# Agent attention and a rational feed-forward block: batch 0's products with v in two halves of TensorE's columns, w_out's second quarter decoded later, and the last decoding step of w_out on GpSimd

## The chip, the cores and the metric

The kernel runs on one core of a Trainium2 chip. The metric is the device time of one execution in microseconds; lower is better. The engines are named as the profile names them: PE (matrix products; PEld its weight loads), DVE (VectorE), ACT (ScalarE), POOL (GpSimd) and SP (it only issues DMAs here). PSUM is the memory that PE writes its products to.

## The reference

```python
def _attn_ref(q, k, v, agents):              # B=2, N=12480, C=128, 49 agents
    def sm(a, b):
        s = scale * (a @ b.transpose(0, 2, 1))
        e = np.exp(s - s.max(-1, keepdims=True))
        return e / (e.sum(-1, keepdims=True) + 1e-09)
    agent_v = sm(agents, k) @ v              # 49 x 128 for each batch
    return sm(q, agents) @ agent_v

def _moe_ref(x, w_in, w_out, a, b):          # x: 24960 x 128, d_ff = 2048
    h = x @ w_in
    P = a[0] + a[1]*h + a[2]*h**2 + a[3]*h**3
    Q = 1.0 + abs(b[0])*abs(h) + abs(b[1])*h**2
    return (P / (Q + 1e-6)) @ w_out
```

q, k, v and agents are float32; w_in and w_out are float64, and the kernel turns them into float32 on the chip.

## The kernel before

**Two parts.** A first part (0 to about 57 us of the profiled execution) finds agent_v of batch 0 and decodes three quarters of the weights. Then every engine reads `flag` and branches into `main`, which runs all tokens of both batches through attention and the feed-forward block (to 1235 us), and does batch 1's agent_v beside it.

**agent_v of batch 0.** The 12480 keys are 98 chunks of 128, in groups g of 10 (the last has 8). PE makes the scores, DVE the maxima, ACT the exponentials S. `pv_pe` multiplies a group's chunks with v (49 x 129, the last column a sum) and adds them up in PSUM: groups 0 to 4 into `bank[4]` (HG = 5), 5 to 9 into `bank[5]`, which have different maxima; L863 scales the first by `fac`, L866 adds the second. `av_norm` (L289 to L291) divides, PE transposes (L294), ACT and DVE copy the result into `avt` (L297, L298). Each float32 product is two PE instructions in the profile.

**Decoding the weights.** A quarter is 512 columns, ("i", 0..3) of w_in, ("o", 0..3) of w_out. `decode` gives four steps: two ACT instructions (L177, L178), three of DVE (L181 to L183: t, t, s), two of POOL (L186: r = r * s; L187: r = r + t), and a last one of DVE (L190: dst = (z >= TINY2) * r). `ORDER` lists the loads on SP's queue among those of v and q, `DECS` the group after which a quarter is decoded; `dec` issues the last step of a quarter only after the first steps of the next one (`pend`). Quarters ("o", 0) and ("o", 1) fall in the stretch of agent_v; ("o", 2) and ("o", 3) are decoded in `main` by `w_stream`. In the branch taken here (`fast`), POOL also multiplies each quarter of w_out by a coefficient Kg (`w_scale`, L680).

**The attention of the first 1024 tokens** stands in the same stretch: scores after g = 2, exponentials, sums, `q_split` on POOL (L441 to L443), and the transposes `q_tr` on PE (L448) after g = 7.

**main.** x is never formed: m = agent_v * w_in (L301) is rounded to a high part by ACT (L304) and a rest by DVE (L309), and h is made from the attention weights and the two parts of m (L495, L496 on PE) in units of 3 x (128 of d_ff x 512 tokens). A unit then takes ACT (L560 and, for two units together, a logarithm and an exponential L574, L576), DVE (L589, L581), POOL (L601, a DMA that adds a constant from `omd` to u; L643, a product) and PE (L503, product with w_out) seven units later. `omd` is filled once at main's start: POOL writes a tile (L610), SP sends it (L611). The attention of later tokens, the decoding of ("o", 2) and ("o", 3) and batch 1 are cut into pieces that `attend` puts between the units. Up to unit 7 PE runs dummy products (L657).

**What sets the order.** The order on each engine is that in which the code issues; waits are by semaphores. A core's engines each work strictly through their own list.

## Time and profile before

| | us |
|---|---|
| three executions | 1233.75, 1234.26, 1234.34 (median 1234.26) |
| the profiled execution | 1236.99, of which its span 1235.2 |
| PE busy | 1203.0 (97%) |
| DVE, ACT, POOL busy | 1109.9 (90%), 1139.0 (92%), 1092.1 (88%) |

The span runs from the first to the last instruction of the profiled execution. PEclk, where it stands, is the granted clock of TensorE as a share of full speed: 1.00 is 2.4 GHz, 0.50 is 1.2 GHz.

### The profile page before, as it was taken

How to read it: one execution, taken by the hardware profiler on the slowest of the kernel's cores; microseconds unless marked ns; L12 is line 12 of the kernel's file. 1: busy time of each engine (PE TensorE's matmuls, PEld its weight loads, DVE VectorE, ACT ScalarE, POOL GpSimd, SP SyncE). 2: the span in 40 equal slices, each digit the busy share in tenths (PEclk: the TensorE clock that was granted, in tenths of full speed). 3: DMA queues.
4: the chain of work that ended last, by engine and by line, in shares of the span. 5: the costliest groups of instructions: out<-in, count | busy, mean ns of one | idle time of the engine just before them, and what ended most of it. 6: DMA issues, size and time to landing. Idle time of an engine off the chain costs nothing.

```text
span 1235.2 us, 14434 instructions
## 1 busy us (share of the span) xinstructions
PE 1203.0 (97%) x5396; PEld 706.7 (57%) x5396; DVE 1109.9 (90%) x876; ACT 1139.0 (92%) x717; POOL 1092.1 (88%) x544
## 2 busy tenths in 40 slices
PE   7979999999999999999999999999999999999998
PEld 7845555555555555555556555555555555555554
DVE  6898898988988888888989999999999998999996
ACT  3489999999999999999999999999999999999994
POOL 4549979798999989989798999999899998999993
PEclk8989999999999999999999999999999999999999
DMA  9569999898999989999899989999999989999991
GB/s 357 225 150 203 200 226 224 191 230 182 210 204 215 230 192 213 207 212 199 169 188 187 207 178 203 191 204 200 190 197 192 218 164 194 196 211 176 202 198 36
DMA packets 55312, 246.17 MB, mean 199 GB/s; under 512 B 4800, under 2 KB 5312, under 8 KB 55232
## 3 DMA queue, kind: packets, MB, share of 16 engines
q0 software_dynamic: 32768, 188.75, 79.5%
q1 hardware_dynamic: 22464, 56.39, 12.8%
q8 instruction: 45, 0.74, 0.2%
q14 instruction: 35, 0.29, 0.1%
HBM read 231.56 MB, written 13.57 MB: 198 GB/s over the span
## 4 chain that ended last, share of the span: by engine, by line
PE 63%; DVE 17%; DMA 6%; POOL 5%; issue 4%; ACT 4%; SPq 0%; DVEq 0%; ACTq 0%; POOLq 0%
PE outb L503 36%; PE slot L495 11%; PE slot L496 10%; DVE w L589 7%; DVE u L581 6%; POOL u L643 4%; DMA u<-omd 4%; ACT u L560 3%; PE outb L214 2%; DMA k<-kT 2%; PE outb L448 1%; PE outb L272 1%; ACT w L576 1%; POOL u L601 1%; DMA v<-vP 1%
## 5 line engine op out<-in xcount | busy, mean ns | idle before, releaser
L643 POOL TENSOR_TENSOR u<-u,w 128x1536 f32<-128x1536 f32 x240 | 906.4, 3985 | 14.5 <-DMA u<-omd 13.8
L503 PE MATMUL outb<-u,wo 128*128 128x512 f32 (+1 forms) x1568 | 712.9, 590 | 2.8 <-DVE av_two L278 1.3
L589 DVE SCALAR_TENSOR_TENSOR w<-slot,cf,u 128x1536 f32<-128x1536 f32 (+1 forms) x262 | 472.1, 1802 | 86.4 <-ACT u L560 66.6
L581 DVE SCALAR_TENSOR_TENSOR u<-u,cf,slot 128x1536 f32<-128x1536 f32 (+1 forms) x262 | 472.2, 1802 | 9.3
L503 PEld LDWEIGHTS outb<-u,wo 128*128 128x128 f32 x1568 | 295.3, 189 | 278.1 <-issue 242.4
L560 ACT ACTIVATE u<-slot 128x1536 f32<-128x1536 f32 (+1 forms) x262 | 380.0, 1451 | 44.1 <-PE slot L496 18.0
L495 PE MATMUL slot<-pT,m_hi 113*128 113x512 f32 (+3 forms) x800 | 370.5, 464 | 11.5 <-DVE u L581 10.5
L574 ACT ACTIVATE w<-w,cf 128x3072 f32<-128x3072 f32 (+1 forms) x134 | 374.3, 2795 | 0.5 <-DVE w L589 0.5
L576 ACT ACTIVATE w<-w 128x3072 f32<-128x3072 f32 (+1 forms) x134 | 361.9, 2703 | 0.0
L496 PE MATMUL slot<-pT,m_lo 113*128 113x512 f32 (+3 forms) x800 | 312.6, 392 | 0.0
L495 PEld LDWEIGHTS slot<-pT,m_hi 113*128 113x128 f32 x800 | 151.0, 189 | 88.2 <-DVE u L581 38.5
L601 POOL DMA_DIRECT2D u<-omd x112 | 158.5, 1415 | 31.0 <-DVE u L581 15.2
L496 PEld LDWEIGHTS slot<-pT,m_lo 113*128 113x128 f32 x800 | 151.8, 190 | 49.4 <-issue 25.3
L448 PEld LDWEIGHTS outb<-ident,p 128*113 128x113 f32 x187 | 26.2, 177 | 27.8 <-issue 14.7
L646 POOL COPY turn<-u 1x1 f32<-1x1 f32 x17 | 4.1, 241 | 41.4 <-DVE u L594 41.4
L594 DVE SCALAR_TENSOR_TENSOR u<-u,cf,w 128x1536 f32<-128x1536 f32 (+2 forms) x22 | 38.2, 1758 | 0.0
L214 PEld LDWEIGHTS outb<-ag,q 128*64 128x64 f32 x748 | 24.3, 140 | 18.1 <-issue 13.5
L448 PE MATMUL outb<-ident,p 128*113 128x128 f32 x187 | 28.7, 276 | 2.8 <-POOL p L443 2.3
L441 POOL TENSOR_TENSOR e<-e,qs 128x392 f32<-128x392 f32 (+1 forms) x25 | 29.6, 1183 | 0.1
L442 POOL TENSOR_SCALAR p<-e 128x392 fp32r<-128x392 f32 (+1 forms) x25 | 29.5, 1180 | 0.1
L214 PE MATMUL outb<-ag,q 128*64 128x49 f32 x748 | 27.3, 227 | 0.0
L186 POOL TENSOR_TENSOR r<-r,s 128x512 f32<-128x512 f32 x6 | 9.3, 1556 | 19.6 <-DVE s L183 19.6
(137 smaller groups left out, 520.1 us busy)
## 6 DMA issues: line engine op xcount, KB each, us to landing
u<-omd POOLq DMA_DIRECT2D x112, 1536.0 KB, 12.3
q<-qT SPq DMA_DIRECT2D x24, 512.0 KB, 8.6
outT<-o SPq DMA_DIRECT2D x48, 256.0 KB, 5.9
u<-omd POOLq DMA_DIRECT2D x16, 768.0 KB, 8.3
v<-vP SPq DMA_DIRECT2D x24, 258.0 KB, 8.3
k<-kT SPq DMA_DIRECT2D x24, 256.0 KB, 7.6
v<-vP SPq DMA_DIRECT2D x9, 645.0 KB, 11.4
k<-kT SPq DMA_DIRECT2D x8, 640.0 KB, 9.5
```

Of the source, the lines that this page charges most:

```text
L214: PE.matmul(bank[lo:hi, o:o + A], lhsT=toks[:, lo:hi], rhs=ag[:, b * A:(b + 1) * A], start=True, stop=True)
L448: PE.transpose(bank[:KR, c * CH:(c + 1) * CH], t[:, h * 4 + c, :].bitcast(F32), ident[:CH, :CH])
L495: PE.matmul(s[:, j, lo:hi], lhsT=m_hi[b][:KR, f], rhs=rhs, start=True, stop=False)
L496: PE.matmul(s[:, j, lo:hi], lhsT=m_lo[b][:KR, f], rhs=rhs, start=False, stop=True)
L503: PE.matmul(outs[blk % 2][:, :width(blk)], lhsT=wo[:, fc, :], rhs=g[:, j, :], start=fc == 0, stop=fc == NFC - 1)
L560: ACT.activation(out=x, in_=h, func=AF.Square, scale=arm["xb"], bias=1.0)
L574: ACT.activation(out=r, in_=r, func=AF.Ln, bias=arm["lb"])
L576: ACT.activation(out=r, in_=r, func=AF.Exp, scale=-1.0)
L581: DVE.scalar_tensor_tensor(out=y, in0=x, scalar=co["kap_l"], in1=h, op0=ALU.add, op1=ALU.mult)
L589: DVE.scalar_tensor_tensor(out=w, in0=h, scalar=co["mu_l"], in1=x, op0=ALU.max, op1=ALU.add)
L601: POOL.dma_start(out=t, in_=omd.unsqueeze(1).to_broadcast([128, 2, UJ * BT]), accum_op=ALU.add)
L643: POOL.tensor_tensor(out=view("u", g), in0=view("u", g), in1=view("w", g), op=ALU.mult)
```

## The change

It has four parts. (1) `pv_pe` puts a group's products by turns into partitions 0 to 48 and 64 to 112 of the PSUM bank, which are two halves of PE's columns (LO = 64). To join the two sums, `pv_up` (DVE) copies partitions 64 to 112 into `av_two`, and `pv_down` (PE, a product with the identity) adds the copy to partitions 0 to 48. For `bank[4]` the copy is issued after g = 4, the product after g = 5; for `bank[5]` both stand at the end, with ten dummy products (DUP) on PE between them. (2) ("o", 1) is loaded after v's last groups, and decoded after g = 9, with its DVE and POOL steps issued only after the copies into `avt`. (3) `dec` issues the last step of a quarter ahead of the next quarter's DVE steps, where it stood behind them. (4) The last step of all four quarters of w_out runs on POOL as two instructions (L191, L192 of the changed kernel). For quarters 2 and 3 the first of them takes the factor Kg, so that their w_scale is gone; quarters 0 and 1 keep theirs.

```diff
-WARM, DUM, DUA = 8, 2, 4
+WARM, DUM, DUA, DUP = 8, 2, 4, 10
 ORDER = (... ("v", 5), ("o", 0), ("v", 6),
-         ("o", 1), ("v", 7), ("v", 8), ("v", 9), ("q", 1))
+         ("v", 7), ("v", 8), ("v", 9), ("o", 1), ("q", 1))
-DECS = ((-5, "i", 0), (-3, "i", 1), (1, "i", 2), (3, "i", 3), (5, "o", 0), (7, "o", 1))
+DECS = ((-5, "i", 0), (-3, "i", 1), (1, "i", 2), (3, "i", 3), (5, "o", 0), (9, "o", 1))
...
         def end():
+            if on_pool:
+                POOL.tensor_scalar(out=z, in0=z, scalar1=TINY2, scalar2=scale, op0=ALU.is_ge, op1=ALU.mult)
+                POOL.tensor_tensor(out=dst, in0=z, in1=r, op=ALU.mult)
+                return
             DVE.scalar_tensor_tensor(out=dst, in0=z, scalar=TINY2, in1=r, op0=ALU.is_ge, op1=ALU.mult)
...
-            PE.matmul(bank[:A, :C + 1], lhsT=S[:, g * G + c, :], rhs=vt[:, c, :], start=first and c == 0, stop=last and c == n - 1)
+            o = c % 2 * LO
+            PE.matmul(bank[o:o + A, :C + 1], lhsT=S[:, g * G + c, :], rhs=vt[:, c, :], start=first and c < 2, stop=last and c == n - 1)
+
+    def pv_up(bank):
+        DVE.tensor_copy(out=av_two[LO:KR, :], in_=bank[LO:KR, :C + 1])
+
+    def pv_down(bank):
+        PE.matmul(bank[:A, :C + 1], lhsT=ident[LO:KR, LO:KR], rhs=av_two[LO:KR, :], start=False, stop=True)
...
+        dst = [wo.rearrange("p a b -> p (a b)")[:, h * WP:(h + 1) * WP] for h in (2, 3)]
+        decs = [decode(raw[h], *tmp[h], dst[h], True, co["Kg"] if fast else 1.0) for h in range(2)]
...
         for h in range(2):
-            yield (None, None, [("DVE", lambda bk, f=decs[h][3]: f())] + ([("POOL", lambda bk, h=h: w_scale(h + 2))] if fast else []))
+            yield (None, None, [("POOL", lambda bk, f=decs[h][3]: f())])
...
-                for f in now:
-                    f()
+                a()
                 pend.pop()()
-                pend.append(end)
+                if late:
+                    pend.append(lambda: (d(), p(), end()))
+                else:
+                    d()
+                    p()
+                    pend.append(end)
...
+                if g in (HG - 1, ng - 1):
+                    pv_up(bank[4 if g < HG else 5])
                 if g == HG:
+                    pv_down(bank[4])
                     DVE.tensor_scalar(out=av_acc, in0=bank[4][:A, :C + 1], scalar1=fac, scalar2=None, op0=ALU.mult)
                 load_next(g)
             assert not wanted and not decs
+            for _ in range(DUP):
+                PE.matmul(outs[0][:, :128], lhsT=ident, rhs=ident, start=True, stop=True)
+            pv_down(bank[5])
             DVE.tensor_tensor(out=av_acc, in0=bank[5][:A, :C + 1], in1=av_acc, op=ALU.add)
```

Lines below L190 move: L264 is L269 in the changed kernel, L448 is L459, L441 to L443 are L452 to L454, L610 and L611 are L621 and L622, L680 is L691, L643 is L654, L863 and L866 are L882 and L888.

**Place one, DVE in the stretch of agent_v.** `bank_110` is `bank[4]`, `bank_111` is `bank[5]`; `raw_326` is ("i", 3), `raw_208` ("o", 0), `raw_235` ("o", 1). DVE before:

```order
L181 TENSOR_SCALAR t_442<-raw_326 128x512
L182 SCALAR_TENSOR_TENSOR t_442<-raw_326,t_442 128x512
L183 TENSOR_SCALAR s_443<-t_442 128x512
L190 SCALAR_TENSOR_TENSOR wi<-z_373,r_372 128x512
L181 TENSOR_SCALAR t_370<-raw_208 128x512
L182 SCALAR_TENSOR_TENSOR t_370<-raw_208,t_370 128x512
L183 TENSOR_SCALAR s_371<-t_370 128x512
L190 SCALAR_TENSOR_TENSOR wi<-z_445,r_444 128x512
L863 TENSOR_SCALAR av_acc<-bank_110,fac_547 49x129
L181 TENSOR_SCALAR t_442<-raw_235 128x512
L182 SCALAR_TENSOR_TENSOR t_442<-raw_235,t_442 128x512
L183 TENSOR_SCALAR s_443<-t_442 128x512
```

DVE from the same step of ("i", 2) on now, where L194 is the old L190, L272 the copy `pv_up`, and L882 and L888 the old L863 and L866:

```order
L194 SCALAR_TENSOR_TENSOR wi<-z_373,r_372 128x512
L181 TENSOR_SCALAR t_442<-raw_326 128x512
L182 SCALAR_TENSOR_TENSOR t_442<-raw_326,t_442 128x512
L183 TENSOR_SCALAR s_443<-t_442 128x512
L272 COPY av_two<-bank_110 49x129
L194 SCALAR_TENSOR_TENSOR wi<-z_445,r_444 128x512
L181 TENSOR_SCALAR t_370<-raw_208 128x512
L182 SCALAR_TENSOR_TENSOR t_370<-raw_208,t_370 128x512
L183 TENSOR_SCALAR s_371<-t_370 128x512
L882 TENSOR_SCALAR av_acc<-bank_110,fac_546 49x129
L272 COPY av_two<-bank_111 49x129
L888 TENSOR_TENSOR av_acc<-bank_111,av_acc 49x129
```

The copy of the first bank stands behind the last step of ("i", 2) (L194, z_373) and the three DVE steps of ("i", 3). After L882 only the second copy stands ahead of the sum; the steps of ("o", 1) have left this place.

**PE at the same place.** L269 are the products with v (`v_5_332` is group 5, the last four groups 6 to 9), L275 is `pv_down`, L459 the transposes `q_tr`, L886 and L891 dummies. PE now:

```order
L269 MATMUL bank_110<-v_4_330,S 49x129 x10
L269 MATMUL bank_111<-v_5_332,S 49x129 x10
L275 MATMUL bank_110<-av_two,ident 49x129
L269 MATMUL bank_111<-v_0_262,S 49x129 x10
L269 MATMUL bank_111<-v_1_289,S 49x129 x10
L459 MATMUL bank_107<-ident,p_95 113x128 x4
L459 MATMUL bank_109<-ident,p_95 113x128 x4
L269 MATMUL bank_111<-v_2_324,S 49x129 x10
L269 MATMUL bank_111<-v_3_328,S 49x129 x8
L886 MATMUL outb_70<-ident 128x128 x10
L275 MATMUL bank_111<-av_two,ident 49x129
L891 MATMUL outb_70<-ident 128x128 x4
```

Before, the same list had neither L275 nor L886. The first L275, which needs DVE's copy of `bank[4]`, stands between the products of g = 5 and of g = 6; the second stands behind the dummy products, with only the older four dummies after it.

**Place two, POOL from the end of the first part into main.** r_372 is ("o", 0), r_444 is ("o", 1). POOL before:

```order
L186 TENSOR_TENSOR r_444<-r_444,s_443 128x512
L187 TENSOR_TENSOR r_444<-r_444,t_442 128x512
L895 TENSOR_LOAD flag
L896 COMPARE_AND_BRANCH
L610 TENSOR_SCALAR w_750<-ident,cf 128x1536
L680 TENSOR_SCALAR wo<-wo,cf 128x512 x2
L601 DMA u_744<-omd 128x2x1536
```

POOL now, with L191 and L192 the new last step, L621 the tile that fills `omd`:

```order
L191 TENSOR_SCALAR z_373<-z_373 128x512
L192 TENSOR_TENSOR wo<-z_373,r_372 128x512
L186 TENSOR_TENSOR r_444<-r_444,s_443 128x512
L187 TENSOR_TENSOR r_444<-r_444,t_442 128x512
L191 TENSOR_SCALAR z_445<-z_445 128x512
L192 TENSOR_TENSOR wo<-z_445,r_444 128x512
L917 TENSOR_LOAD flag
L918 COMPARE_AND_BRANCH
L621 TENSOR_SCALAR w_766<-ident,cf 128x1536
L691 TENSOR_SCALAR wo<-wo,cf 128x512 x2
L612 DMA u_760<-omd 128x2x1536
```

The two last steps of POOL have come in ahead of the tile that fills `omd`, and the first two steps of ("o", 1) now wait for DVE steps that stand behind the copies into `avt`.

**Place three, POOL in the first units of main.** Names of u and w are main's tiles; e and p are the attention weights of the second 1024 tokens. POOL before:

```order
L601 DMA u_745<-omd 128x2x1536
L680 TENSOR_SCALAR wo<-wo,cf 128x512
L643 TENSOR_TENSOR u_744<-u_744,w_749 128x1536
L441 TENSOR_TENSOR e_96<-e_96,qs_865 128x8x49
L680 TENSOR_SCALAR wo<-wo,cf 128x512
L601 DMA u_746<-omd 128x2x1536
L643 TENSOR_TENSOR u_744<-u_744,w_749 128x1536
L442 TENSOR_SCALAR p_95<-e_96 128x8x49
L443 TENSOR_TENSOR p_95<-e_96,p_95 128x8x49
```

POOL now, with L191 and L192 the last steps of ("o", 2) and ("o", 3):

```order
L612 DMA u_761<-omd 128x2x1536
L191 TENSOR_SCALAR u_763<-u_763,cf 128x512
L192 TENSOR_TENSOR wo<-u_763 128x512
L654 TENSOR_TENSOR u_760<-u_760,w_765 128x1536
L452 TENSOR_TENSOR e_96<-e_96,qs_881 128x8x49
L191 TENSOR_SCALAR w_768<-w_768,cf 128x512
L192 TENSOR_TENSOR wo<-w_768 128x512
L612 DMA u_762<-omd 128x2x1536
L654 TENSOR_TENSOR u_760<-u_760,w_765 128x1536
L453 TENSOR_SCALAR p_95<-e_96 128x8x49
L454 TENSOR_TENSOR p_95<-e_96,p_95 128x8x49
```

In the place of one w_scale for each of the quarters 2 and 3 stand two instructions, ahead of p.

## Rows read from the trace of the kernel before

**Rows 1.** The page: busy us, share of span, instructions

```profile
PE 1203.0 (97%) x5396; PEld 706.7 (57%) x5396; DVE 1109.9 (90%) x876; ACT 1139.0 (92%) x717; POOL 1092.1 (88%) x544
```

**Rows 2.** Windows: us, busy of PE, PEld, DVE, ACT, POOL, PEclk, DMA share, GB/s

```profile
65.20:67.30 2.10, 0.00 (x0) 0.00 (x0) 2.06 (x3) 0.00 (x0) 0.00 (x0) 1.00 0.64 265
67.80:71.10 3.30, 3.30 (x30) 2.36 (x30) 3.00 (x2) 1.16 (x1) 0.00 (x0) 0.50 0.00 0
78.70:81.30 2.60, 0.00 (x0) 0.00 (x0) 2.56 (x3) 2.60 (x5) 1.76 (x2) 1.00 1.06 217
81.40:84.70 3.30, 3.30 (x7) 2.48 (x8) 3.20 (x5) 3.30 (x2) 1.63 (x2) 0.50 0.34 69
100.00:1200.00 1100.00, 1090.24 (x4528) 625.46 (x4526) 1005.88 (x723) 1062.69 (x627) 1025.45 (x469) 1.00 0.97 200
```

**Rows 3.** The chain that ended last: start us, us on the chain, what

```profile
50.63 1.18 DVE t L181
...
54.54 0.21 DVE av_acc L866
...
100.55 0.44 PE outb L448 x4
...
354.22 0.58 PE outb L272 x8
```

**Rows 4.** Timeline of PE, 37 to 55 us: start, us, instructions

```profile
37.92 11.23 PE L264 MATMUL bank<-v,S 128*49 128x129 f32 x100
49.08 1.13 PE L448 MATMUL bank<-ident,p 128*113 128x128 f32 x8
50.14 4.18 PE L264 MATMUL bank<-v,S 128*49 128x129 f32 x36
```

**Rows 5.** Timeline of POOL and DVE, 38 to 56 us

```profile
41.39 1.28 POOL L187 TENSOR_TENSOR r<-r,t 128x512 f32<-128x512 f32 x1
42.81 0.85 POOL L441 TENSOR_TENSOR e<-e,qs 128x392 f32<-128x392 f32 x1
44.67 1.01 POOL L443 TENSOR_TENSOR p<-e,p 128x392 fp32r<-128x392 f32 x1
...
38.43 0.69 DVE L182 SCALAR_TENSOR_TENSOR t<-raw,t 128x512 int32<-128x512 int32 x1
39.16 0.43 DVE L183 TENSOR_SCALAR s<-t 128x512 int32<-128x512 int32 x1
42.99 1.21 DVE L182 SCALAR_TENSOR_TENSOR t<-raw,t 128x512 int32<-128x512 int32 x1
44.79 1.44 DVE L190 SCALAR_TENSOR_TENSOR wi<-z,r 128x512 f32<-128x512 f32 x1
55.15 0.60 DVE L291 TENSOR_SCALAR av_acc<-av_acc,avr,cf 49x128 f32<-49x128 f32 x1
```

**Rows 6.** Timeline of main's start, and the line of the omd transfer

```profile
56.34 0.21 DVE L298 COPY avt<-bank 128x49 f32<-128x49 f32 x1 [0.59 <-ACT avt L297]
58.17 1.55 POOL L610 TENSOR_SCALAR w<-ident,cf 128x1536 f32<-128x1536 f32 x1 [1.16 <-PE outb L301]
71.48 1.82 DVE L589 SCALAR_TENSOR_TENSOR w<-slot,cf,u 128x1536 f32<-128x1536 f32 x1 [0.64 <-ACT u L560]
...
DMA to landing us min/median/max: 7.8/7.8/7.8
```

**Rows 7.** Timeline of DVE, POOL and PE, 87 to 100 us

```profile
87.06 0.64 DVE L190 SCALAR_TENSOR_TENSOR wo<-u 128x512 f32<-128x512 f32 x1
91.19 1.28 DVE L190 SCALAR_TENSOR_TENSOR wo<-w 128x512 f32<-128x512 f32 x1
...
87.81 0.69 POOL L680 TENSOR_SCALAR wo<-wo,cf 128x512 f32<-128x512 f32 x1 [1.03 <-DVE wo L190]
99.10 0.97 POOL L443 TENSOR_TENSOR p<-e,p 128x392 fp32r<-128x392 f32 x1
...
96.30 0.50 PE L495 MATMUL slot<-pT,m_hi 113*128 113x512 f32 x1 [1.59 <-DVE u L581]
```

More of the change, by code (lines that the diff above doesn't have):

```diff
@@ L70 @@
 QPE, QTR = 2, 7
-WARM, DUM, DUA = 8, 2, 4
+WARM, DUM, DUA, DUP = 8, 2, 4, 10
 BETWEEN = {0: 1, 1: 1, 2: 1, 3: 2}
-ORDER = (("i", 0), ("i", 1), ("v", 0), ("v", 1), ("q", 0), ("i", 2), ("v", 2), ("i", 3), ("v", 3), ("v", 4), ("v", 5), ("o", 0), ("v", 6), ("o", 1),
-         ("v", 7), ("v", 8), ("v", 9), ("q", 1))
-DECS = ((-5, "i", 0), (-3, "i", 1), (1, "i", 2), (3, "i", 3), (5, "o", 0), (7, "o", 1))
+ORDER = (("i", 0), ("i", 1), ("v", 0), ("v", 1), ("q", 0), ("i", 2), ("v", 2), ("i", 3), ("v", 3), ("v", 4), ("v", 5), ("o", 0), ("v", 6),
+         ("v", 7), ("v", 8), ("v", 9), ("o", 1), ("q", 1))
+DECS = ((-5, "i", 0), (-3, "i", 1), (1, "i", 2), (3, "i", 3), (5, "o", 0), (9, "o", 1))
 @with_exitstack
@@ L170, in load_w, with decode @@
         SP.dma_start(out=raw, in_=src.bitcast(I32).rearrange("p (f w) -> p f w", w=2)[:, h * WP:(h + 1) * WP, :])
-    def decode(raw, t, s, r, z, dst):
+    def decode(raw, t, s, r, z, dst, on_pool=False, scale=1.0):
         lo, hi = raw[:, :, 0], raw[:, :, 1]
@@ L699, in w_stream @@
             load_w(raw[h], w_out, h + 2)
-        decs = [decode(raw[h], *tmp[h], wo.rearrange("p a b -> p (a b)")[:, (h + 2) * WP:(h + 3) * WP]) for h in range(2)]
+        dst = [wo.rearrange("p a b -> p (a b)")[:, h * WP:(h + 1) * WP] for h in (2, 3)]
+        decs = [decode(raw[h], *tmp[h], dst[h], True, co["Kg"] if fast else 1.0) for h in range(2)]
         for act, dve, pool, _ in decs:
@@ L784, in load_next, with dec @@
                         load_w(raws[kind, h], {"i": w_in, "o": w_out}[kind], h)
-            def dec(kind, h):
+            def dec(kind, h, late=False):
                 ts = [ring(sp, 2, [128, WP], dt, nm) for nm, dt in (("t", I32), ("s", I32), ("r", F32), ("z", F32))]
                 dst = wi if kind == "i" else wo.rearrange("p a b -> p (a b)")
-                *now, end = decode(raws[kind, h], *ts, dst[:, h * WP:(h + 1) * WP])
-                for f in now:
-                    f()
+                a, d, p, end = decode(raws[kind, h], *ts, dst[:, h * WP:(h + 1) * WP], kind == "o")
+                a()
                 pend.pop()()
-                pend.append(end)
+                if late:
[4 more added lines that the diff above has]
+                    pend.append(end)
                 used.add((kind, h))
@@ L799, in dec_at @@
                 while decs and decs[0][0] == when:
-                    dec(*decs.pop(0)[1:])
+                    dec(*decs.pop(0)[1:], late=not decs)
             ops, late = coefs()
```

## The prediction

> **What bounds the kernel now.** I begin with the busy shares of the page [rows 1]: PE 97%, and no other engine above 92%. A mean says little, so I cut the span by windows. From 100 to 1200 us PE is busy for 1090.24 of 1100.00 us at a granted clock of 1.00 [rows 2]. The part of a microsecond that is lost there is spread out, and nothing in the diff changes what PE does after the ramp. So the time is "when PE enters its steady run" plus a constant, and whatever moves that point moves the end one for one. The question is what leads to it.
>
> The chain of waits answers that in two places. In the stretch of agent_v it runs on DVE: decoding of ("o", 1) from 50.63, behind it the last step of ("o", 0), and behind that the sum of the two banks at 54.54 [rows 3]. PE was nearly as late: its last products run from 50.14 for 4.18 us, to 54.32 [rows 4]. Two engines thus end within 0.2 us of each other, and a change must make both earlier. In main's ramp the chain is on DVE again (units' steps, with decoding steps between them) up to PE's first product of the unit at 96.30, which waited 1.59 us for DVE [rows 7]. Then PE takes over and comes to the transposes L448 on the chain at 100.55 [rows 3]; their p came from POOL at 99.10 + 0.97 = 100.07 [rows 7]. A third engine is half a microsecond from the chain there.
>
> **How DVE and POOL share.** Before costing steps I look at what DVE and POOL do to each other. L182 takes 0.69 us alone and 1.21 us beside POOL's L441: POOL runs 42.81 to 43.66, DVE ends at 44.20, 0.54 later. L190 started at 44.79 ends at 46.23, 0.55 after POOL's L443 (45.68) [rows 5]. So a decoding step of DVE and a step of POOL do not run at the same time; the one waits for most of the other. Work moved from DVE to POOL is not work moved away from DVE's time altogether.
>
> The Trainium skill says this as a rule: the page "Perfetto Trace Analysis", section "Optimizing Scalar/DVE Operations", notes that offloading between these two might not help, since they share an SBUF port. The trace agrees with the sharing (0.69 against 1.21 us). By the rule taken strictly, DVE's gain in the ramp below would be nothing, PE's wait there 0.9 instead of 2.7 us and without loss of clock, and the sum +4.8 instead of +5.6.
>
> **Part one: the products with v.** 100 instructions in 11.23 us are 0.112 each, two to a product, 0.224 [rows 4]. The same alternation already exists in batch 1: L272 has 8 instructions (4 products) on the chain for 0.58 us [rows 3]; unpaired they would be 0.90, so a pair costs one product's 0.224 and a visit 0.13 more (0.58 - 2 x 0.224). A group of 10 becomes 5 x 0.224 + 0.13 = 1.25 us instead of 2.24. Taken by itself PE would gain about 1 us a group.
>
> But PE now meets a wait. `pv_down` of bank[4] stands in PE's list behind group 5 and needs DVE's copy, which in DVE's list stands behind the last step of ("i", 2) and three steps of ("i", 3). The last step of ("i", 2) needs POOL's L187, which ended at 41.39 + 1.28 = 42.67 [rows 5] and comes some 0.3 us later now, since one DVE step has moved ahead of the steps that feed it: 43.0. Behind L187 POOL goes on with q_split, 0.85 to 1.01 us each, right beside DVE's four steps. Alone these are 0.69, 0.43, 0.69 and 0.43 (L182 and L183 [rows 5], the last step taken as L182, L181 as L183), 2.2 us, and the copy, from PSUM, 0.21 as L298 [rows 6]: 45.4. If each of three POOL steps delays one, they end about 0.55 after it: 47.3. The rows above are of the very same POOL steps beside the same DVE steps, so I take 47.0.
>
> PE reaches that wait early: the rows count 50 products from 37.92 [rows 4], groups 3 to 7; three groups at 1.25 bring it to 41.7 at the latest. So it idles for 5 us or more. What remains for it at 47.0: pv_down with its hand-over 0.35 (two instructions and a drain, an estimate from the 0.112 and 0.13), groups 6 and 7 10 x 0.224 + 0.13 = 2.37, transposes 1.06 (49.08 to 50.14 [rows 4]), groups 8 and 9 9 x 0.224 + 0.13 = 2.15, in all 5.9 at full clock, to 52.9. Then ten dummies, 20 instructions at 0.112 = 2.24, and the second pv_down with its hand-over 0.3: 55.5. That is with the clock at full.
>
> After an idle stretch it was not. PE stood for 2.10 us and 2.60 us, and each time the granted clock of the next 3.30 us is 0.50 [rows 2]; after the 1.59 us at 96.30 [rows 7] it stayed: the transposes at 100.55 take 0.11 each [rows 3], the rate of the products above. Idling 5 us lies on the far side of both. Over 3.3 to 4 us at half speed PE loses 1.65 to 2.0 us: I take 1.85, so the sum starts at 57.35 instead of 54.54, +2.8. av_norm's L291, 0.60 us beside POOL, falls to about 0.25 as POOL is idle then (an estimate near L298's 0.21; at most 0.60): -0.35. **The copies into avt come 2.5 us later.** Bounds: the clock kept, +0.6 (0.96 - 0.35); 47.3 for the copy and 4.5 us at half clock, +3.5. DVE by itself would have been ready at about 51.5 (below).
>
> The Trainium skill, "TensorE: Matmul & The Clock Gate", Part 1, says the observation behind the gate runs free of the kernel, so that one kernel counted 6, 11 or 14 slow products in different runs; no run here shows that, and by it the loss would vary from run to run about the value above.
>
> **Part two: ("o", 1) behind the copies.** Before, 56.34 (DVE's copy, call it s) was followed at 58.17, s + 1.8, by POOL's tile for omd of 1.55 us; the transfer takes 7.8 us [rows 6]. It landed before anything needed it: the tile buffer is next written by DVE's unit 2 at 71.48 = s + 15.1 [rows 6], while 58.17 + 1.55 + 7.8 = 67.5. Now POOL has first to do, after the copy (0.21) and three DVE steps (1.55): L186 and L187 at 1.28 each, L191 (as L680, 0.69), L192 1.28 and gaps of 0.2, so its tile starts at s + 6.5, is written at s + 8.05, sent 0.5 later, and lands at s + 16.4. Unit 2 would come at s + 16.4 instead of s + 15.1: **+1.3**. ACT's first unit, which in the changed program also waits for that POOL step, starts at about s + 6.6, a delay below 1 us that the 1.3 contains. Bounds: +0.3 (POOL steps at 1.2 and the transfer a little faster) to +1.3; the sum uses the row durations.
>
> **Parts three and four in the ramp.** The two L190 of quarters 2 and 3 leave DVE: 0.64 + 1.21 (91.19, without its overlap with the step ahead) [rows 7], -1.85 us on the DVE chain. On POOL each w_scale of 0.69 [rows 7] becomes 0.69 + 1.28 (L191 as L680, L192 as L187), +2.56 and 0.1 of gaps; POOL loses its wait of 1.03 for DVE [rows 7] and some 0.3 of delay beside the two L190. So p comes 1.3 us later, at 101.4 where it was 100.07, while PE, fed 1.85 earlier by DVE, would be there at 98.7. It waits 2.7 us, and the transposes start 0.9 to 1.0 us later than 100.55: **+1.0**. Bounds: -1.85 if POOL found the time elsewhere; +1.8 if its idle time does not come back.
>
> That new wait of 2.7 us is as long as those that halved the clock [rows 2], and longer than the 1.59 that didn't. At half clock 3.30 us do the work of 1.65: 0 to +1.7; I take half of it, **+0.8**, since the engine may make it up while DVE feeds it.
>
> **Sum.** 2.5 + 1.3 + 1.0 + 0.8 = +5.6 us. In the profiled execution the time is 1236.99 with 1.8 outside the span, 2.73 above the median; both are shifted alike, so I add to the median: 1234.26 + 5.6 = 1239.9, given as 1240.0. Adding the bounds: 0.6 + 0.3 - 1.85 + 0 = -1.0 to 3.5 + 1.3 + 1.8 + 1.7 = +8.3, that is 1233.3 to 1242.6; the likeliest case's own range is 1236.7 to 1242.6.
>
> **Rivals.** What can be told from no change here is 0.2%, 2.47 us: 1231.8 to 1236.7.
>
> *No change that can be measured.* The clock survives PE's stall (which shrinks if POOL's steps don't delay DVE), and the tile's lateness is hidden: 0.6 + 0.3 to 1.3 + 0 to 1.0, +0.9 to +2.9 with a middle of 1.8: 1236.0. For it: each single term has its lower bound there. Against: two stalls of 2.10 and 2.60 us did halve the clock.
>
> *Faster.* DVE alone is the bound in both places and PE follows. Then the decoding of ("o", 1) and the last step of ("o", 0), from 50.63 to 54.54, leave the path; the second copy costs 0.2 and the sum starts about 51.5, -3.0. The ramp gives back 1.85 and the tile costs 1.3: -3.5, 1230.8. It needs PE to have finished its last product by about 49, so that the dummies and pv_down end at 51.5: with 5.9 us left behind the wait, the first copy must be done by about 43. POOL's L187 ends at 42.67, and four steps stand between; this decides it. Before, the chain on DVE speaks for it; that PE ended at 54.32 itself speaks against.
>
> **How the numbers follow.** Forecast (slower by over 0.2%) 0.64, no change 0.24, faster 0.12. The predicted time is that of the forecast. The range is 1232.0 to 1242.5: it leaves out most of the faster case (0.10) and a tail of the slower one (0.08).
>
> **What would show it.** In the changed profile: PE idle from about 41 until DVE's first L272 copy, which ends near 47; clock 0.50 after it; the sum L888 near 57 and the copies into avt near 59; POOL's tile at 6.5 us after them; PE waiting for POOL's p near 105 to 107. I am wrong if the first copy of bank[4] ends before 44 or the clock stays at 1.00 behind the stall (then the rivals), or if POOL's p is not what the transposes wait for (then the third term is -1.85 instead of +1.0).

## The result and the profile after

The changed kernel takes 1250.38 us (median of 6, 1249.12 to 1256.85), the kernel before 1234.14 us beside it (1233.37 to 1234.47): a ratio of 1.0138, 95% interval 1.0121 to 1.0154. It is slower by 16.2 us by the medians and by 17 us by the ratio, as forecast in direction, and by three times the 5.6 us that were forecast. The profiled execution took 1250.69 us, span 1248.9, which is 13.7 above that of before.

The two chains are compared at marks that both kernels have. The table holds start times (us) from the timelines of DVE and PE: the copy into avt on DVE (L298, now L309), the first DVE step of units 0, 2, 5 and 6 (L589, now L600), and the first transposes after the ramp (L448, now L459).

| | copy into avt | unit 0 | unit 2 | unit 5 | unit 6 | transposes | span |
|---|---|---|---|---|---|---|---|
| before | 56.34 | 63.59 | 71.48 | 87.62 | 92.58 | 100.38 | 1235.2 |
| after | 59.91 | 69.65 | 79.41 | 95.00 | 105.88 | 115.37 | 1248.9 |
| later by | 3.57 | 6.06 | 7.93 | 7.38 | 13.30 | 14.99 | 13.7 |

So 3.6 us are lost up to the copies, 4.4 more up to unit 2, 5.4 more up to unit 6, 1.7 more up to the transposes, 15.0 in all. Followed further by the same DVE step, the lateness is 16.4 us at unit 100 (541.43 against 525.01 us), close to the 16.2 of the medians, and 13.5 at unit 220: between the two the profiled execution of before lost time of its own, with PE waiting 1.86 us for p at 1041.87, a wait that the changed kernel's profile does not have. So 13.7 is what these two executions differ by; the change is nearer to 15 or 16. The steady part is what it was: the window of 1100 us behind the transposes (columns as in [rows 2]) has PE busy for 1091.17, where [rows 2] has 1090.24.

```profile
47.50:51.00 3.50, 3.50 (x30) 3.11 (x32) 1.08 (x3) 0.00 (x0) 2.27 (x2) 0.50 0.05 18
109.60:112.60 3.00, 3.00 (x7) 2.42 (x8) 2.96 (x2) 0.04 (x1) 2.92 (x4) 0.50 0.99 203
115.50:1215.50 1100.00, 1091.17 (x4534) 626.55 (x4533) 1005.91 (x724) 1062.93 (x627) 1023.02 (x468) 1.00 0.97 200
```

The first two of these windows show half clock (0.50) behind two idle stretches of PE. The first stretch is the stall in front of the first joining product. This is the timeline of PE and DVE there, which answers to [rows 4] and [rows 5]:

```profile
43.30 1.31 DVE L194 SCALAR_TENSOR_TENSOR wi<-z,r 128x512 f32<-128x512 f32 x1 [0.34 <-POOL r L187]
47.13 0.30 DVE L272 COPY av_two<-bank 49x129 f32<-49x129 f32 x1
...
47.48 0.66 PE L275 MATMUL bank<-av_two,ident 49*49 49x129 f32 x2 [5.41 <-DVE av_two L272]
48.07 4.22 PE L269 MATMUL bank<-v,S 128*49 128x129 f32 x40
...
53.29 2.19 PE L269 MATMUL bank<-v,S 128*49 128x129 f32 x36
55.41 2.50 PE L886 MATMUL outb<-ident 128*128 128x128 f32 x20
57.84 0.42 PE L275 MATMUL bank<-av_two,ident 49*49 49x129 f32 x2
...
58.30 0.29 DVE L888 TENSOR_TENSOR av_acc<-bank,av_acc 49x129 f32<-49x129 f32 x1 [2.47 <-PE bank L275]
```

The reader should see three things: PE idle for 5.41 us until DVE's copy, which stands behind L194 and three more decoding steps (43.30 to 47.13, beside GpSimd's q_split), while L194 itself waited only 0.34 us for GpSimd's L187; the 40 product instructions behind the stall taking 4.22 us, where 36 of the same kind take 2.19 us a little later; and the dummies standing on the path, since the sum waits 2.47 us for PE.

The start of main, answering to [rows 6]: GpSimd, ACT, DVE, and the line of the omd transfer.

```profile
64.87 1.92 POOL L191 TENSOR_SCALAR z<-z 128x512 f32<-128x512 f32 x1
66.88 1.26 POOL L192 TENSOR_TENSOR wo<-z,r 128x512 f32<-128x512 f32 x1
68.32 1.55 POOL L621 TENSOR_SCALAR w<-ident,cf 128x1536 f32<-128x1536 f32 x1 [0.18 <-POOL wo L192]
...
68.17 1.45 ACT L571 ACTIVATE u<-slot 128x1536 f32<-128x1536 f32 x1 [3.27 <-POOL wo L192]
...
69.65 1.82 DVE L600 SCALAR_TENSOR_TENSOR w<-slot,cf,u 128x1536 f32<-128x1536 f32 x1 [3.97 <-ACT u L571]
79.41 1.82 DVE L600 SCALAR_TENSOR_TENSOR w<-slot,cf,u 128x1536 f32<-128x1536 f32 x1 [2.51 <-DMA omd<-w]
...
DMA to landing us min/median/max: 9.3/9.3/9.3
```

ACT's first unit waits 3.27 us for quarter 1's last step on GpSimd, and unit 2 then waits for the omd transfer as well. L191, a one-input instruction, takes 1.92 us; the old w_scale of the same shape took 0.69 [rows 7].

The ramp, answering to [rows 7]: GpSimd from 94 us, DVE's unit 6, and PE behind it.

```profile
94.81 1.99 POOL L191 TENSOR_SCALAR u<-u,cf 128x512 f32<-128x512 f32 x1
96.88 1.28 POOL L192 TENSOR_TENSOR wo<-u 128x512 f32<-128x512 f32 x1
98.12 3.48 POOL L654 TENSOR_TENSOR u<-u,w 128x1536 f32<-128x1536 f32 x1
101.56 0.84 POOL L452 TENSOR_TENSOR e<-e,qs 128x392 f32<-128x392 f32 x1
102.50 1.99 POOL L191 TENSOR_SCALAR w<-w,cf 128x512 f32<-128x512 f32 x1
104.58 1.26 POOL L192 TENSOR_TENSOR wo<-w 128x512 f32<-128x512 f32 x1
...
111.07 0.96 POOL L454 TENSOR_TENSOR p<-e,p 128x392 fp32r<-128x392 f32 x1
...
105.88 1.82 DVE L600 SCALAR_TENSOR_TENSOR w<-slot,cf,u 128x1536 f32<-128x1536 f32 x1 [7.26 <-POOL wo L192]
...
109.60 0.79 PE L506 MATMUL slot<-pT,m_hi 113*128 113x512 f32 x1 [7.55 <-DVE u L592]
```

Unit 6 of DVE stands for 7.26 us until L192 of quarter 3 ends (104.58 + 1.26 = 105.84). The tile names tell why: quarter 3's L191 reads and writes a main tile named w (order rows of place three: w_768). Quarter 3 keeps its temporaries in the tile into which units 6 and 7 write their w. Before, DVE did that last step itself, just ahead of its unit 6 (91.19 [rows 7]); now it stands on GpSimd behind quarter 2's last step, the 3.48 us of unit 0's product, and L452.

### The profile page after: what moved, and what is told of

Read it like the earlier page. It is cut to its first block, busy times and chain, and to the rows that moved or that the text cites. A ratio compares the mean times of both kernels' runs of the same rounds, so it can differ in the third digit from the quotient of the medians.

```text
span 1248.9 us, 14482 instructions
## 1 busy us (share of the span) xinstructions
PE 1200.8 (96%) x5420; PEld 702.2 (56%) x5420; DVE 1102.7 (88%) x874; ACT 1138.5 (91%) x717; POOL 1100.9 (88%) x550
## 4 chain that ended last, share of the span: by engine, by line
PE 69%; DVE 17%; ACT 5%; issue 3%; POOL 3%; DMA 1%; SPq 0%; DVEq 0%; POOLq 0%; ACTq 0%
PE outb L514 39%; PE slot L506 12%; PE slot L507 11%; DVE w L600 7%; DVE u L592 6%; ACT u L571 3%; PE outb L218 2%; ACT w L587 2%; PE outb L459 2%; POOL u L654 1%; PE outb L283 1%; DMA omd<-w 1%; PE bank L269 1%; DMA k<-kT 1%; PE bank L218 1%
## 5 line engine op out<-in xcount | busy, mean ns | idle before, releaser
L654 POOL TENSOR_TENSOR u<-u,w 128x1536 f32<-128x1536 f32 x240 | 906.1, 4007 | 2.2 <-DMA u<-omd 1.6
L600 DVE SCALAR_TENSOR_TENSOR w<-slot,cf,u 128x1536 f32<-128x1536 f32 (+1 forms) x262 | 471.9, 1801 | 98.8 <-ACT u L571 72.9
L459 PEld LDWEIGHTS outb<-ident,p 128*113 128x113 f32 x187 | 26.3, 177 | 24.9 <-issue 16.9
L452 POOL TENSOR_TENSOR e<-e,qs 128x392 f32<-128x392 f32 (+1 forms) x25 | 31.8, 1271 | 0.0
L459 PE MATMUL outb<-ident,p 128*113 128x128 f32 x187 | 28.6, 275 | 0.4
L454 POOL TENSOR_TENSOR p<-e,p 128x392 fp32r<-128x392 f32 (+1 forms) x25 | 25.0, 1001 | 2.1
```

The lines of the kernel that those rows point to most:

```text
L459: PE.transpose(bank[:KR, c * CH:(c + 1) * CH], t[:, h * 4 + c, :].bitcast(F32), ident[:CH, :CH])
L600: DVE.scalar_tensor_tensor(out=w, in0=h, scalar=co["mu_l"], in1=x, op0=ALU.max, op1=ALU.add)
L654: POOL.tensor_tensor(out=view("u", g), in0=view("u", g), in1=view("w", g), op=ALU.mult)
```

## The experiments

The kernels ran in later sessions than the result above, with the kernel before beside them; its single times there lie between 1232.8 and 1240.0, so single times of one kernel differ by more than in the result, and I read the profiled executions by their marks and the times by their ratios. Marks of all runs in which they carry an argument, from the same timelines:

| | copy into avt | unit 0 | unit 2 | unit 5 | unit 6 | transposes |
|---|---|---|---|---|---|---|
| all last steps on DVE | 59.09 | 69.33 | 76.50 | 92.66 | 97.64 | 105.44 |
| quarters 2, 3 on DVE | 58.69 | 68.44 | 77.96 | 94.10 | 99.08 | 106.88 |
| own tile for quarter 3 | 59.77 | 69.52 | 79.10 | 94.68 | 98.21 | 111.81 |
| halves alone | 58.70 | 65.95 | 73.11 | 89.23 | 94.21 | 102.01 |
| ends on GpSimd alone | 55.59 | 64.55 | 72.92 | 88.53 | 99.45 | 110.32 |
| late join | 56.01 | 66.35 | 75.89 | 91.46 | 102.36 | 111.72 |
| late join and two on DVE | 56.12 | 66.46 | 76.09 | 92.25 | 97.21 | 105.01 |
| halves alone, late join | 59.00 | 67.66 | 74.82 | 90.94 | 95.90 | 103.70 |
| late join, ends on DVE | 59.74 | 70.07 | 77.23 | 93.36 | 98.34 | 107.84 |
| the same in the old order | 52.28 | 64.92 | 72.09 | 88.24 | 93.21 | 101.01 |

**All last steps back on DVE.**

```diff
-                a, d, p, end = decode(raws[kind, h], *ts, dst[:, h * WP:(h + 1) * WP], kind == "o")
+                a, d, p, end = decode(raws[kind, h], *ts, dst[:, h * WP:(h + 1) * WP])
...
-        decs = [decode(raw[h], *tmp[h], dst[h], True, co["Kg"] if fast else 1.0) for h in range(2)]
+        decs = [decode(raw[h], *tmp[h], dst[h]) for h in range(2)]
...
-            yield (None, None, [("POOL", lambda bk, f=decs[h][3]: f())])
+            yield (None, None, [("DVE", lambda bk, f=decs[h][3]: f())] + ([("POOL", lambda bk, h=h: w_scale(h + 2))] if fast else []))
```

> The changed kernel with the last decoding step of all four quarters of w_out on DVE again (and GpSimd's w_scale of quarters 2 and 3 back). Theory: of the 15 us by which the changed kernel's transposes in the ramp are late (115.5 against 100.6 us), 3.6 come from agent_v (DVE's copy into avt at 59.9 instead of 56.3), 4.4 from the tile that fills omd, which waits for four GpSimd steps of quarter 1 of which one takes 1.95 us, 5.4 from unit 6's first DVE step waiting for GpSimd's last step of quarter 3, and 1.7 from TensorE's half clock behind that wait. With the steps back on DVE the last two must vanish and the second shrink to 1 or less: 1238 to 1240. Rival: the time is lost to DVE and GpSimd sharing a port all through the ramp, whoever does the last step: then 1246 or more.

Measured: 1245.63 us (1240.63 to 1248.08), ratio 1.0085 (1.0058 to 1.0112); the profiled execution, 1240.63, is the fastest of the four. Unit 6 no longer waits for GpSimd: it comes 4.98 us after unit 5 (before 4.96, changed 10.88). The second term did not fall to 1 or less: unit 0 comes 10.24 us after the copies, where it was 7.25 before, so quarter 1's decoding behind the copies costs 3 us at unit 0, and 2.3 at unit 2 (17.41 against 15.14), with no last step on GpSimd. The median lies above what was expected and 0.4 us below the rival's 1246, so the time does not decide between the two. The trace does, for the execution that it shows: the transposes come 9.9 us earlier than in the changed kernel. As it is that of the fastest execution, what the other three lost is open.

**Only quarters 2 and 3 back on DVE** (the second and third hunk above).

> The changed kernel with only quarters 2 and 3 decoded to the end on DVE again (with GpSimd's w_scale). Theory: the 5.4 and 1.7 us of unit 6's wait are gone, the 3.6 and 4.4 remain: 1241 to 1243, with the omd transfer still ending near 79 us and unit 6's first DVE step 8 us later than in the kernel before. Rival (the ramp's loss is the sharing of the port by quarter 1's late decoding): 1246 or more.

Measured: 1243.36 us (1242.06 to 1244.83), ratio 1.0057 (1.0038 to 1.0077). The transposes come at 106.88 instead of 115.37, 8.5 us earlier, of which 1.2 are there at the copies. As expected, unit 2 still waits for the omd transfer (2.27 us), and unit 6 stands where its predecessors put it, 6.5 us later than before (expected 8):

```profile
77.96 1.82 DVE L600 SCALAR_TENSOR_TENSOR w<-slot,cf,u 128x1536 f32<-128x1536 f32 x1 [2.27 <-DMA omd<-w]
...
99.08 1.82 DVE L600 SCALAR_TENSOR_TENSOR w<-slot,cf,u 128x1536 f32<-128x1536 f32 x1
```

**Another tile for quarter 3.** The instructions and their order are those of the changed kernel; r and z of quarter 3 lie in tiles of batch 1's v.

```diff
-        second = [(w[3], i) for i in range(4)] if fast else [...]
+        own = [ring(kv, 2, [CK, G1 * (C + 1)], F32, "v1") for _ in range(2)]
+        second = [(w[3], 0), (w[3], 1), (own[0], 0), (own[1], 0)] if fast else [...]
```

> The changed kernel with r and z of quarter 3 in two tiles of batch 1's v, which is loaded later, so that unit 6's w tile is free as soon as GpSimd's L187 is done; the instructions are the same. Theory (DVE waits for the tile, not for time on GpSimd): unit 6's first DVE step starts near 98.7 instead of 105.9, and the next to be waited for is GpSimd's p near 112.0, so the transposes start about 112 instead of 115.4: 1246 to 1248. Rival (the wait is only where the lateness of GpSimd shows, and all else would be late too): 1250.

Measured: 1253.46 us (1251.52 to 1255.87), ratio 1.0148 (1.0117 to 1.0178), so no gain. The mechanism is shown: with the tile free unit 6 starts at 98.21, 7.7 us earlier than in the changed kernel. The price is not what I expected. PE now waits for GpSimd's p, a wait that lay hidden beside the first, and its clock halves at that place instead (the four transposes take 1.20 us, elsewhere 0.60):

```profile
110.81 0.95 POOL L454 TENSOR_TENSOR p<-e,p 128x392 fp32r<-128x392 f32 x1
...
111.81 1.20 PE L459 MATMUL outb<-ident,p 128*113 128x128 f32 x4 [5.63 <-POOL p L454]
```

Two waits of about one length stand side by side; both come from GpSimd being late with its list: p ends at 111.76, where it was 100.07. Taking one away buys little: the transposes start 3.56 us earlier than in the changed kernel, but the half clock now falls behind them, and at unit 10 only 1.0 us is left (122.43 against 123.43). That the times show no gain at all lies within their spread; in the profiled execution PE also waited 1.40 us for p at 921.21.

**Four forms of GpSimd's first instruction.** Quarter 2 runs without the threshold and quarter 3 with another function in its place, so the output is not the reference's.

```diff
-                POOL.tensor_scalar(out=z, in0=z, scalar1=TINY2, scalar2=scale, op0=ALU.is_ge, op1=ALU.mult)
+                if form == 0:     # quarter 0
+                    POOL.tensor_scalar(out=z, in0=z, scalar1=TINY2, scalar2=None, op0=ALU.is_ge)
+                elif form == 2:   # quarter 2
+                    POOL.tensor_scalar(out=z, in0=z, scalar1=TINY2, scalar2=scale, op0=ALU.mult, op1=ALU.mult)
+                elif form == 3:   # quarter 3
+                    POOL.tensor_scalar(out=z, in0=z, scalar1=TINY2, scalar2=scale, op0=ALU.max, op1=ALU.mult)
+                else:             # quarter 1, as in the change
+                    POOL.tensor_scalar(out=z, in0=z, scalar1=TINY2, scalar2=scale, op0=ALU.is_ge, op1=ALU.mult)
```

> The changed kernel with GpSimd's first instruction of the last step in four forms: quarter 0 the comparison alone, quarter 1 comparison and factor as in the change, quarter 2 two factors (the threshold is left out), quarter 3 a maximum and a factor (the threshold is replaced). Theory: the comparison makes it 1.95 us where two factors take 0.69 (the old w_scale): quarters 0 and 1 near 1.9, quarters 2 and 3 near 0.7. Rival A, the instruction is slow because it writes the tile it reads: all four near 1.95. Rival B, because it has two operations and DVE works beside it: quarter 0 near 0.7 to 1.0, the others 1.95.

Measured in one execution, on the timeline of GpSimd, quarters 0 to 3 in order (L192, L198, L194 and L196 are the four forms):

```profile
54.87 1.53 POOL L192 TENSOR_SCALAR z<-z 128x512 f32<-128x512 f32 x1
...
64.27 1.94 POOL L198 TENSOR_SCALAR z<-z 128x512 f32<-128x512 f32 x1
...
94.06 0.68 POOL L194 TENSOR_SCALAR u<-u,cf 128x512 f32<-128x512 f32 x1
...
100.46 2.00 POOL L196 TENSOR_SCALAR w<-w,cf 128x512 f32<-128x512 f32 x1
```

The comparison alone takes 1.53, with the factor behind it 1.94, two factors 0.68, a maximum and a factor 2.00. At the same four places the changed kernel has 1.97, 1.92, 1.99 and 1.99. All four write the tile they read, so that is not it (rival A), and rival B falls too: the single comparison is slow, and two operations can be fast. What is slow on GpSimd is the operation, and not the comparison alone, as I had it: a maximum is as slow. DVE's work beside it is not the reason either: in the changed kernel quarter 3's L191 takes its 1.99 us at 102.50, while DVE stands still (98.62 to 105.88). Unit 6 still waits 6.00 us in this run, with quarter 2's instruction 1.3 us shorter. The Trainium skill, "GPSIMD Engine Reference", section "Engine selection", has one-input instructions roughly at line rate and two-input ones about twice as slow as DVE's. The trace agrees for two inputs (1.28, where DVE's L194 takes 0.69) and is near it for two factors (0.68), but not for a comparison or a maximum, where the measurement decides.

**The halves alone,** on the kernel before: part (1) of the change, all of it, and nothing else.

> The kernel before with the products in two halves of TensorE's columns alone: both copies, both joining products and the ten dummies as in the change, DVE's decoding order and the last steps as before. Theory (the first joining product is a wait for DVE that costs TensorE 5 us and its clock): DVE's copy of the first bank ends near 46.5, TensorE ends its last product near 54.6, the dummies near 57.0, the sum stands at 57.4 instead of 54.5, the copies into avt 2.6 us later, and nothing else changes: 1236.5 to 1237.5 on a chip that gives the kernel before 1234.3. Rival (the halves speed TensorE up and DVE alone sets the end): 1234 or less.

Measured: 1239.49 us (1236.0 to 1241.42, 10 runs), ratio 1.0029 (1.0018 to 1.0040), that is +3.6 us. The sum stands at 57.08, the copies 2.36 us later than before, and this difference runs on to the transposes (102.01, +1.63). PE waits for the same copy:

```profile
46.00 0.66 PE L271 MATMUL bank<-av_two,ident 49*49 49x129 f32 x2 [5.76 <-DVE av_two L268]
46.60 4.49 PE L265 MATMUL bank<-v,S 128*49 128x129 f32 x40
```

So the halves, which make the products twice as fast, lose by themselves. DVE is through quarter 1's decoding at 53.94 and PE through its products at 54.27, about when both were before; the dummies and the second joining product, for which the sum then waits 2.47 us, come on top.

**The last steps on GpSimd alone,** on the kernel before: part (4) of the change, the quarters decoded when and in the order they were.

> The kernel before with the last decoding step of w_out's four quarters on GpSimd alone. Theory: 0.6 us are won on DVE ahead of the sum; the omd tile then waits for four GpSimd instructions of 6.5 us in all and unit 2 comes 2 to 3 us later; unit 6 waits 5.4 us more for quarter 3, TensorE's clock halves behind it (1.7), and 1.3 us come back later: 8 us, 1241 to 1244. Rival (the late decoding of quarter 1 and the stall are what makes GpSimd late in the ramp): under 1238.

Measured: 1245.01 us (1243.6 to 1245.45), ratio 1.0071 (1.0050 to 1.0092), +8.8 us. The copies come 0.75 us earlier than before, unit 2 1.44 later (expected 2 to 3), unit 6 6.87 later:

```profile
99.45 1.82 DVE L593 SCALAR_TENSOR_TENSOR w<-slot,cf,u 128x1536 f32<-128x1536 f32 x1 [7.29 <-POOL wo L192]
```

The wait is as long as in the changed kernel, so neither the late quarter 1 nor the stall makes it. The rival falls.

**The first joining product three groups later.**

```diff
-                if g == HG:
+                if g == ng - 2:
                     pv_down(bank[4])
                     DVE.tensor_scalar(out=av_acc, in0=bank[4][:A, :C + 1], scalar1=fac, scalar2=None, op0=ALU.mult)
```

> The changed kernel with the first joining product (and the scaling of the first bank) three groups later, after group 8, so that TensorE has other products while DVE gets to its copy. Theory: TensorE no longer stalls before group 6; it waits for p before the transposes (near 45.5), ends group 9 before 50, and the sum comes near 53 instead of 58.3, set by DVE's second copy behind quarter 0's decoding; all after it is as late as in the changed kernel, so 5 us less than the changed kernel: 1244 to 1246. Rival (the stall is hidden by DVE and GpSimd, which are as late): 1249 or more.

Measured: 1247.75 us (1246.95 to 1248.51), ratio 1.0098 (1.0078 to 1.0119), which is 4.9 us less than the changed kernel's ratio gives. The sum comes at 53.82 instead of 58.30; PE goes on through the products with 0.67 us of waiting for p:

```profile
46.63 1.13 PE L459 MATMUL bank<-ident,p 128*113 128x128 f32 x8 [0.67 <-POOL p L454]
47.69 1.31 PE L269 MATMUL bank<-v,S 128*49 128x129 f32 x20
...
53.37 0.42 PE L275 MATMUL bank<-av_two,ident 49*49 49x129 f32 x2 [0.57 <-DVE av_two L272]
```

**No dummies** (DUP = 0 in the changed kernel).

> The changed kernel without the ten dummies. Theory: behind the stall TensorE is the bound, so the sum comes 1.8 us earlier (2.43 us of dummies less the 0.6 that DVE's copy takes), 56.5 instead of 58.3, and the time falls by 1.8 us if TensorE's clock stays: 1248 to 1249. Rival (the dummies keep the clock for what follows): m's products at half clock, and no gain: 1250.

Measured: 1248.28 us (1247.61 to 1249.76), ratio 1.0102 (1.0080 to 1.0123). The sum comes at 56.03, 2.3 us earlier, and the copies at 58.50, 1.4 earlier, because L302 now meets GpSimd's L192 and takes 1.19 us. The profiled execution is 1.8 us below that of the changed kernel. What the rival said of the clock is there too: m's first products, two in 2.02 us at 58.85, run at half the rate of the changed kernel's (four in 1.94 at 60.27). But it costs nothing, as unit 0 comes 9.74 us after the copies in both kernels, behind ACT's wait for GpSimd. By the ratios the run is 4.4 us under the changed kernel, by the transposes (113.85) 1.5. The dummies were a small cost in this place.

**Late join on the kernel before, without dummies** (the halves alone, with the hunk of the late join, DUP = 0).

> The kernel before with the products in halves, the first joining product after group 8, no dummies, and the decoding as before. Theory: TensorE ends group 9 near 49.5, but DVE's second copy stands behind quarter 1's and quarter 0's steps (54.5), so the sum comes near 55.3, 0.8 later than before, and m's products run at half clock behind 5 us of idling: +1 to +2 us against the kernel before. Rival (TensorE was the bound of this stretch): 1 us or more faster than before.

Measured: 1239.18 us (1235.64 to 1242.54, 10 runs), ratio 1.0032 (1.0018 to 1.0045), +3.9 us. The sum comes at 56.49 (expected 55.3), the copies 2.66 later than before; PE idles 5.83 us ahead of the second joining product, and then runs at half clock. The rival, that PE was the bound of this stretch, falls: with PE through its products at about 50 us nothing is won, since DVE's second copy stands behind the decoding of quarter 1.

**Late join, all last steps on DVE, no dummies** (hunks of the first and of the late-join experiment).

> The changed kernel with the first joining product after group 8, no dummies, and all last steps on DVE. Theory: the copies into avt near 56, as before; quarter 1's decoding behind them costs 3 us up to unit 0's first DVE step (17.4 us from the copies to unit 2 in the run with the steps on DVE, 15.1 before); unit 6 does not wait for GpSimd: +2 to +4 us against the kernel before. Rival (with stall and GpSimd's steps gone the halves show their gain): equal or faster.

Measured: 1243.23 us (1240.04 to 1245.37), ratio 1.0064 (1.0040 to 1.0087). A miss. I had overlooked that with the last step on DVE quarter 0's L194 stands ahead of the second copy and waits for GpSimd, so that the copies came at 59.74 and not near 56; the 3 us from the copies to unit 0 (10.33 against 7.25) are there.

**The same in DVE's old order, quarter 0's last step behind the copies too.**

```diff
                 a()
-                pend.pop()()
                 if late:
-                    pend.append(lambda: (d(), p(), end()))
+                    prev = pend.pop()
+                    pend.append(lambda: (d(), p(), prev(), end()))
                 else:
                     d()
                     p()
+                    pend.pop()()
                     pend.append(end)
```

> As the run before it, with DVE's old order (a quarter's last step behind the next quarter's first steps), and the last step of quarter 0 behind the copies too. Theory: nothing stands between the scaling of the first bank (50.6) and the second copy, so the sum comes near 51.5 and the copies into avt near 53, 3 us earlier than before; quarter 1's late decoding takes 3 us back: within 1.5 us of the kernel before. Rival (only the last step's place matters): 2 to 3 us slower.

Measured: 1238.38 us (1235.05 to 1240.23), ratio 1.0031 (1.0013 to 1.0049), +3.8 us; the profiled execution is the fastest of the five. The first half is as expected: the copies stand at 52.28, 4.06 us earlier than before. But unit 0 comes at 64.92, 1.33 later than before: 5.4 us go back, not 3. Quarter 1's last step now stands on DVE ahead of the rest of m, waits for GpSimd, and PE waits behind it; by the profile unit 0 then waits for a load as well, which SP issued after that step.

```profile
57.11 0.69 DVE L194 SCALAR_TENSOR_TENSOR wo<-z,r 128x512 f32<-128x512 f32 x1 [2.50 <-POOL r L187]
57.93 1.41 DVE L320 SCALAR_TENSOR_TENSOR m_lo<-outb,mcol,m_hi 113x512 fp32r<-113x512 f32 x2
...
58.73 2.05 PE L312 MATMUL outb<-wi,avt 128*113 128x512 f32 x2 [3.29 <-DVE m_lo L320]
...
64.92 1.82 DVE L600 SCALAR_TENSOR_TENSOR w<-slot,cf,u 128x1536 f32<-128x1536 f32 x1 [2.63 <-DMA k<-kT]
```

**Two parts taken back at once:** the late join, and quarters 2 and 3 on DVE.

> The changed kernel with two of its parts taken back at once: the first joining product after group 8, and the last steps of quarters 2 and 3 on DVE. Theory (the terms are separate and add up): the copies into avt near 56, as before, unit 6 without a wait for GpSimd, and what is left is quarter 1's decoding behind the copies with its GpSimd steps ahead of the omd tile: unit 2 about 4 us later than before, its distance from the copies 19.5 us as in the changed kernel, and +3 to +5 us in all against the kernel before (the changed kernel's +17 less the 10 and the 5 that the two single runs took off gives +2). Rival (the parts hide one another, so that taking both away gives more or less than the sum): equal to the kernel before, or +7 and more.

Measured: 1240.64 us (1237.42 to 1244.32, 10 runs), ratio 1.0034 (1.0016 to 1.0052), +4.2 us. Copies at 56.12, unit 2 19.97 us behind them (changed 19.50, before 15.14), unit 6 without a wait. The single runs took 10 and 4.9 us off 17, and both together 12.8: the terms add up within what the intervals can tell, and what is left is the price of the late quarter 1, with its last step and quarter 0's on GpSimd.

No version beats the kernel before.

## Why the prediction was wrong

The direction held, and the first term came out just above its upper bound of 3.5. The size did not hold: the second term measured three times what I gave it, and the largest loss was a wait that I had not priced at all.

**First term, the copies into avt later by 2.5 us: 3.57 measured,** 0.3 of which are there before the stretch begins (S's subtraction L258 starts at 35.41, before at 35.10): PE, faster through its products, stood idle for 2.55 us up to 31.76 and ran at 0.50 behind it, where before it had no such wait. The mechanism is as told: the copy of the first bank ended at 47.43 (predicted 47.0), PE idled 5.41 us, the clock halved, and the sum waited for PE. The loss at half clock was 1.8 us (4.22 us for what takes 2.4, by 36 in 2.19), near the 1.85 that I took; in the other profiles with this stall the same 40 instructions take 3.69 to 4.54. The late join (copies 3.9 us earlier than in the changed kernel) shows that this stall is the cause. The halves alone do not show it: their copies are 2.36 us later with the stall and 2.66 without it (late join on the kernel before), since there DVE's second copy stands behind quarter 1's steps, and PE, idle until that copy, halves its clock behind it.

**Second term, quarter 1 behind the copies, +1.3: 4.36 measured.** Two sizes were off. I priced L191 as L680, 0.69 us; it takes 1.92 in main's start, the tile for omd started 8.4 us behind the copies and not 6.5, and the experiment with four forms shows that the operation makes the difference. And I called ACT's wait "a delay below 1 us that the 1.3 contains": ACT's first unit waited for quarter 1's last step and unit 0 came 2.5 us late by it, before the omd transfer (9.3 us from issue to landing, not 7.8) added 1.9. At unit 2 two parts of the change add up: quarter 1 late, with all last steps on DVE, costs 2.3 us (17.41 from the copies, before 15.14); the last steps on GpSimd, with quarter 1 in its old place, cost 2.2 (17.33); the changed kernel has both (19.50). The old-order run shows such a delay reached through m.

**Third term, PE waiting for p, +1.0: the step that failed.** I followed the moved last steps only to p, which stands behind them on GpSimd, and took -1.85 us on DVE as a gain. I did not ask who waits for what the step releases. DVE's unit 6 writes the tile that holds quarter 3's temporaries; as long as DVE did the last step, its own order covered that. On GpSimd the step stands behind 4.3 us of other work and takes 3.3 of its own, and unit 6 waited 7.26 us. Less the 1.85 that had left DVE this is +5.4, at a place that I had as a gain. My own wait exists too, hidden beside this one: in the own-tile run PE waited 5.63 us for p, where I had 2.7. Counted from unit 2, p ended there 4.1 us later than before, where I had 1.3; 2.6 of the difference are the two L191 at 1.99 instead of 0.69. The late join run, in which GpSimd's list starts from copies as early as before, still waits 7.28 us there.

**Fourth term, half a halved clock, +0.8: 1.7 measured.** PE stood 7.55 us and ran at 0.50 behind it. My wait of 2.7 us was too short for the reason just given.

That what moves PE's entry into its steady run moves the end one for one held: the lateness is 15.0 us at the transposes and 16.4 at unit 100. But PE stands for 9.8 us in the window of 1100 [rows 2], not for part of a microsecond.

Of the signs that I had named, the stall, the half clock, the sum (58.30) and the copies (59.91) came near where I put them. The transposes did not wait for p, which was to show me wrong; but the -1.85 that I gave for that case was wrong as well.

The rivals: "no change" and "faster" both needed the stall to be harmless, and it was not. The late-join run, where the stall is gone, and the old-order run, where the copies come 4 us earlier than before, show that what stood behind the copies would have eaten even a full gain. By the port rule of the Trainium skill ("Perfetto Trace Analysis", "Optimizing Scalar/DVE Operations": moving work between DVE and GpSimd may not help) the sum would have been 4.8. The trace agrees with its advice, but for another reason than a shared port: the cost was in the operation's length on GpSimd, the same 1.99 us while DVE stood still, and in what queued behind it.

Open: why single times of one kernel spread by up to 8 us in the experiments (all last steps on DVE: 1240.63 to 1248.08), and so how much of a ratio belongs to the change. Against the lateness of the transposes the ratios run from 1.2 us under (ends on GpSimd alone: +8.8 and +9.94) to 6.8 over (own tile: +18.3 and +11.43). The profiles show two waits far behind the ramp that differ between executions. At PE's products with v of batch 1, 480 to 497 us into the span, PE waited 0.20 us before and 0.87 in the changed kernel, but 2.25 us for a load in the halves alone and 2.21 in the late join with ends on DVE, and the clock in the 3.3 us behind was 0.55 and 0.50. And it waited 1.86 us for p at 1041.87 before, 1.40 at 921.21 in the own-tile run and 1.46 at 914.07 with quarters 2 and 3 on DVE. Whether the change makes such waits likelier, no run here tells.

## What to carry to other kernels

When a step moves to another engine, list what it releases as well as what it feeds: tiles that the step was the last to read are waits for whoever writes them next, and an engine that did the step itself never showed that wait. Price an instruction on a new engine by a row with the same operation, not only the same shape and inputs. A faster stretch on one engine was worth nothing here while the engine that joins its results was late; place the join where that engine will have arrived, and look for the next wait behind each one that is removed.

## What the runs showed of the hardware

On GpSimd a 128x512 float32 instruction with one input took 0.68 us with two multiplications, 1.53 with a comparison alone, 1.94 with a comparison and a multiplication, 2.00 with a maximum and a multiplication; with two inputs a product took 1.28. The comparison with a factor took 1.99 also while DVE stood still. Products of 49 columns, put by turns into the two halves of PE's columns, took 2.19 us for 36 instructions, where they took 4.18 in one half [rows 4]. The clock of PE was 0.50 after idle stretches of 5.41 and 7.55 us, for at least the 3.50 and 3.00 us of the windows shown.
